# First batch of a fused attention and SwiGLU kernel: the remainder's normalization gets a chain of its own, and three late pairs move ahead of the last weight block's lead half

## The chip, the core and the metric

The kernel runs on one core of one Trainium2 chip. A core has five engines with instruction queues of their own: PE (matmuls; its weight loads are listed as PEld), DVE (vector work), ACT (activations and copies), POOL (general vector work, and here the DMAs that cast) and SP (DMAs). Each engine takes its queue in order, and they meet at semaphores. Matmuls read SBUF and write PSUM banks. The metric is the time of one execution on the device, in microseconds; lower is better.

## The reference

Linear attention without softmax, an RMS norm per head, and then a SwiGLU feed-forward layer with an RMS norm over the model width in front:

```python
kv = np.einsum('bhsd,bhse->bhde', k, v)          # 8 batches, 8 heads, 576 rows, 64 wide
out = np.einsum('bhsd,bhde->bhse', q, kv)
rms = np.sqrt(np.mean(out * out, axis=-1, keepdims=True) + 1e-06)
attn = out / rms * g_norm
x = attn.transpose(0, 2, 1, 3).reshape(B * S, H * D)      # 4608 x 512
rms = np.sqrt(np.mean(x * x, axis=-1, keepdims=True) + 1e-06)
xn = x / rms * rms_g
g = xn @ w_gate                                           # 512 x 1536
silu = g * (1.0 / (1.0 + np.exp(-g)))
return silu * (xn @ w_val) @ w_out                        # 1536 x 512
```

Inputs and output are float32; the kernel multiplies in bfloat16.

## The kernel before

The 576 rows of a batch are cut into 512 main rows (four chunks of 128, numbered 0 to 3) and a remainder of 64 rows (chunk NC = 4). The feed-forward layer runs over nine groups of 512 rows: the main rows of each of the eight batches, and one group `xr` that gathers the eight remainders. A group has twelve hidden blocks j of 128; each takes a gate product (`wg`), a silu on ACT, a val product (`wv`) and a multiply on DVE that gives `h`. Then come the products with `wo`. Both norms are merged into one factor for each row and head, `al`: a matmul with `sel` sums squares into `st`, and a chain of twelve small DVE steps (`chain`, lines 455 to 488: u, r, t, srow, z, y, then two rounds of nt, nt, al) turns the sums into the factor by an inverse square root from a bit trick (y) and two Newton rounds. `xna` is the product of attention output and factor; `xT_mm` turns it by matmuls with the identity, and `xT_out` copies it into `x` (main chunks) or `xr` (remainder).

The weights of gate and val are loaded in four blocks of three j each (`FB`), by DMAs of POOL's queue in the order wg0, wv0, wg1, wv1 up to wv3. Behind them POOL issues loads of batch 1, the four `wo` loads and loads of batch 2.

The first batch is written out by hand, in program order, with no planner. Columns of x stand for rows of the batch. Its first two chunks (256 columns, the lead half) are prepared first. Then a list `early` of 22 slots runs all of the lead half's gate and val products, and behind each slot n a function `behind(n)` (line 861) issues a piece of the work that prepares the rest of the batch, chunks 2, 3 and the remainder:

- slot 0: the gates of j 0 to 2 together; slots 1 to 3: their vals.
- slots 4 to 6 gates and 7 to 9 vals of weight block 1; 10 to 12 and 13 to 15 of block 2; 16 to 18 and 19 to 21 of block 3.
- behind 0 and 1 the transposes of q (`qT_mm`, `qT_out`; the remainder at 1); behind 2 to 4 the transposed output and its square (`oT_mm`, `sqT_`); behind 5 and 6 the sums (`stat_pairs`), all into one tile; behind 6 to 10 the twelve chain steps (`steps`) over chunks 2 to 4 at once; behind 8 to 10 the output itself (`o_pairs`); behind 12, 13 and 15 `xna`; behind 15, 16 and 18 the transposes of x and the copies on ACT.

After the list come twelve slots that each hold gate and val of one j for the late half (columns 256 to 511), and then sixteen slots of products with `wo`. The attention of batch 1 is put behind these by slot number (`place_second`, with its first argument after the planner as the slot of its k-v product); later batches and groups are placed by a planner with costs (`Placer`). Gate and val products of one slot after another rotate through three PSUM banks (`mm1`): a gate's bank is free when its silu has been taken, a val's when its h has been made.

Line 641 is the matmul of gate and val, 669 that of the first gates, 308 the transposes of q, 380 `oT_mm`, 405 the sums, 350 `o_pairs`, 520 the transposes of x, 530 and 542 the copies of x on ACT, 360 `xna`, 650 silu, 659 h, 215 the cast of the remainder of q on POOL, 466 to 484 the chain.

Of the kernel before, what the change touches and what calls it, by code (L numbers as in the profile page):

```python
# [86 lines left out]
def kernel(  # L87
# [17 lines left out]
    NC = 4  # L105
    MAIN = 128 * NC
    REM = S - MAIN
    NS = d_model // 128
    NF = d_ff // 128
    FB = (3, 3, 3, 3)  # L110
# [21 lines left out]
    o2_p = pool("o2", 2, space=bass.MemoryType.PSUM)  # L132
    att_p = pool("att", 3, space=bass.MemoryType.PSUM)
# [454 lines left out]
    def place_second(P, s):  # L588
        a = Att(1)
        V, A = nc.vector, nc.scalar  # L590
        ps = {}
        pe = lambda at, cost, n, fn: P.at("PE", cost, lambda: ps.__setitem__(n, fn()), s + at)
        dve = lambda at, cost, fn: P.at("DVE", cost, fn, s + at)
        act = lambda at, cost, fn: P.at("ACT", cost, fn, s + at)

        def turn_q():
            for n, (js, chunks) in enumerate(((P0, range(NC)), (P1, range(NC)), (ALL, (NC,)))):
                ps[n] = a.qT_heads(js, chunks)

        P.at("PE", 1.2, turn_q, s - 4)  # L600
        for j in range(2):
            dve(-3 + j, 0.42, lambda j=j: a.qT_out(ps[0][:, j : j + 1], (j,), 0, V))
            act(-3 + j, 0.58, lambda j=j: a.qT_out(ps[1][:, j : j + 1], (2 + j,), 0, A))
        act(-1, 0.58, lambda: a.qT_out(ps[2], ALL, NC, A))
        P.at("PE", 1.14, lambda: a.kv_mm(range(NS)), s)
        dve(1, 0.43, lambda: a.kv_half(0))
        dve(1, 0.43, lambda: a.kv_half(1))

        parts = [((j,), 0, NC) for j in range(NS)] + [(ALL, NC, NC + 1)]
        for n in range(NC + 1):  # L610
            pe((2, 2, 3, 4, 5)[n], 0.25, ("oT", n), lambda n=n: a.oT_mm(*parts[n]))
            act((3, 4, 4, 5, 6)[n], 0.62, lambda n=n: a.sqT_(ps["oT", n], *parts[n]))
        act(6, 1.28, lambda: A.preload_act_table(ACT.Sqrt))
        P.at("PE", 0.64, lambda: a.stat_mm(0, NC + 1), s + 6)
        for n in range(NC + 1):
            P.at("PE", 0.24, lambda n=n: a.o_mm(n, mm1_p if n == 2 else None), s + (7, 7, 8, 9, 10)[n])
        dve(7, 2.2, lambda: a.lead_chain(0, NC + 1, True))
        for c in range(NC + 1):
            dve(9 + c, 0.68, lambda c=c: a.xna_(c, V, a.o[c]))
        for at, js, cs in ((11, P0, (0, 1)), (13, P1, (0, 1)), (14, P0, (2, 3)), (15, P1, (2, 3))):  # L620
            P.at("PE", 0.24, lambda js=js, cs=cs: a.xT_mm(js, cs), s + at)
            for j in js:
                dve(at + 1, 0.3, lambda j=j, cs=cs: a.xT_out(j, cs, V))
        P.at("PE", 0.15, lambda: a.xT_mm(ALL, (NC,)), s + 16)
        dve(17, 0.62, lambda: [a.xT_out(j, (NC,), V) for j in ALL])
        P.floor = s + 18
        return s + 18
# [24 lines left out]
    def gate_of(g, j, c0=0, c1=MAIN):  # L652
        silu_of(g, j, mm1(g, wg, j, c0, c1), c0, c1)
# [7 lines left out]
    def slots_a(g, j, c0=0, c1=MAIN):  # L661
        return [Slot("gate", lambda: gate_of(g, j, c0, c1)), Slot("val", lambda: val_of(g, j, c0, c1))]

    def gates(g, js, c0, c1):
        ps = [mm1_p.tile([128, MAIN], FP32, name="mm1")[:, : c1 - c0] for _ in js]
        for s in range(NS):
            for p, j in zip(ps, js):
                n, jj = where[j]
                nc.tensor.matmul(
                    p, lhsT=wg[n][:, s, jj * 128 : (jj + 1) * 128], rhs=x_of(g, s, c0, c1), start=s == 0, stop=s == NS - 1  # L670
                )
        for p, j in zip(ps, js):
            silu_of(g, j, p, c0, c1)
# [61 lines left out]
    def slots_b_by_j(g):  # L735

        box = {}
        order = [(j, t) for j in range(NF) for t in range(4)]

        def part(n):  # L740
            if n == 0:
                for t in range(4):
                    p = o2_p if t < 2 else mm1_p
                    box[t] = p.tile([128, d_model], FP32, name="o2" if t < 2 else "mm1")
            for j, t in order[BJ * n : BJ * (n + 1)]:
                mm2(box[t], g, j, t)
            if n == 4 * PARTS - 1:
                for t in (2, 3, 0, 1):
                    store(g, t, box[t], nc.vector if t == 3 else nc.scalar)

        return [Slot("all", lambda n=n: part(n)) for n in range(4 * PARTS)]
# [12 lines left out]
    V, G, A = nc.vector, nc.gpsimd, nc.scalar  # L764
    H0, H1 = (0, 4), (4, 8)
    P0, P1 = (0, 1), (2, 3)
    ALL = range(NS)
# [32 lines left out]
    a = Att(0)  # L800
# [49 lines left out]
        f()  # L850

    half = MAIN // 2
    early = [Slot("half", lambda: gates(0, range(FB[0]), 0, half))]
    for n, w in enumerate(FB):
        js = range(FB0[n], FB0[n] + w)
        early += [slots_a(0, j, 0, half)[0] for j in js if n] + [slots_a(0, j, 0, half)[1] for j in js]
    held = {}

    steps = {6: (0, 3), 7: (3, 5), 8: (5, 8), 9: (8, 10), 10: (10, 12)}

    def behind(n):
        if n == 0:
            ps = a.qT_mm(ALL, (2, 3))
            a.qT_out(ps[:, 0:2], P0, 2, V)
            a.qT_out(ps[:, 2:4], P1, 2, V)
        elif n == 1:
            a.qT_out(a.qT_mm(ALL, (NC,)), ALL, NC, A)
        elif n in (2, 3):
            js = (P0, P1)[n - 2]
            a.sqT_(a.oT_mm(js, 2, 4, o2_p), js, 2, 4)  # L870
        elif n == 4:
            a.sqT_(a.oT_mm(ALL, NC, NC + 1, o2_p), ALL, NC, NC + 1)
        elif n == 5:
            a.st = None
            a.stat_pairs(P0, 2, 4, att_p, "att")
            a.stat_pairs(P1, 2, 4, att_p, "att")
        elif n == 6:
            a.stat_pairs(ALL, NC, NC + 1, att_p, "att")
        if n in steps:
            for f in a.chain(2, NC + 1)[slice(*steps[n])]:  # L880
                f()
        if n in (8, 9):
            held[n - 8] = a.o_pairs((P0, P1)[n - 8], 2, 4, att_p, "att")
        elif n == 10:
            held[2] = a.o_pairs(ALL, NC, NC + 1, o2_p, "o2")
        if n in (12, 13):
            i = (12, 13).index(n)
            a.xna_pairs(held[i], (P0, P1)[i], 2, 4)
        elif n == 15:
            a.xna_pairs(held[2], ALL, NC, NC + 1)  # L890
        if n in (15, 16):
            i = (15, 16).index(n)
            a.xT_mm((P0, P1)[i], (2, 3), None if i else o2_p)
            for j in (P0, P1)[i]:
                a.xT_out(j, (2, 3), A)
        elif n == 18:
            a.xT_mm(ALL, (NC,))
            for j in ALL:
                a.xT_out(j, (NC,), A)
# [11 lines left out]
    gate = load_q(2)  # L911
    tc.add_manual_dep(gate.ins, wo_loads[0].ins.name, SYNC, reason="the weights come first")

    def one(two):
        return Slot("half", lambda: [s.run() for s in two])

    slots = [one(slots_a(0, j, half, MAIN)) for j in range(NF)] + slots_b_by_j(0)
    starts = [0]
    for g in (*range(1, B - 1), B, B - 1):
        starts.append(len(slots))  # L920
        slots += [s for j in range(NF) for s in slots_a(g, j)] + slots_b(g, g == B - 1)
    P = Placer(slots, 3)
    casts = ()
    for b in range(1, B):
        if b == 1:
            end = place_second(P, 9)
        else:
            s0 = starts[b - 1]
            end = place_attention(P, b, casts, s0 - 2, s0 + 2 * NF - 4)
        if os.environ.get("PLACER"):  # L930
            print("batch", b, "to", end, "wanted at", starts[b], "casts", casts)
        else:
            assert end < starts[b] + (b == 1), (b, end, starts)
        if b == 1:
            for n, at in ((0, 6), (1, 24), (2, 30), (3, 40)):
                for j in range(NS):
                    for w, eng, cost in ((wg, "DVE", 0.09), (wv, "ACT", 0.13)):
                        f = P.put(eng, cost * FB[n], lambda w=w, n=n, j=j, e=eng: fold(w[n], j, e), at=starts[1] + at + j)
                        assert f[1] < starts[2] + (2 * FB0[n] if n == 3 else 0), f
            casts = place_casts(P, 2, starts[1] - 9)  # L940
        elif b + 1 < B:
            P.put("SP", 0.0, lambda b=b: load_q(b + 1), at=starts[b - 1] + 6 * (b == 2))
            casts = place_casts(P, b + 1, starts[b - 1] + 18)
            for n, f in enumerate(loads_kv(b + 1)):
                if b == 2:
                    P.at("POOL", 0.85, f, starts[1] + 11 + n)
                else:
                    P.put("POOL", 0.85, f, at=starts[b - 1] + 14)
# [29 lines left out]
```

## Time and profile before

| | |
|---|---|
| median of 3 runs | 325.04 us (324.96 to 325.22) |
| profiled execution | 324.99 us, span 323.2 us, granted clock 1.000 |
| busy | PE 312.9 us, DVE 178.7, ACT 143.1, POOL 89.3 |
| span of the list `early`, from its first matmul | 17.41 to 31.86 us |
| the fourth late pair's gate starts | 34.48 us |

Times of an instruction are microseconds from the start of the span. The timeline's rows read: start, time taken by the merged run of equal instructions, engine, line, operation, what is written and read, form, count, and in brackets how long the engine sat idle before and what ended that. Matmuls overlap: the time between starts is the pace, and the time taken is longer. The chain of waits follows the last instruction back to what released it; its rows read start, time, what.

### The profile page before, as it was taken

To read this page: it belongs to the slowest core of one execution; us is meant where nothing else is said; L and a number is where in the kernel's file an instruction comes from. 1 tells how busy PE (TensorE), PEld (TensorE's weight loads), DVE (VectorE), ACT (ScalarE), POOL (GpSimd) and SP (SyncE) were. 2 spreads that over 40 slices of the span, in tenths; PEclk is the share of its full clock that TensorE was granted. 3 is DMA by queue.
4 is the path that set the end of the run, shared out by engine and by line. 5 is a ranking of instruction groups with operands and counts; after the bars stand their busy time and mean duration, and the time that the engine had idled before them with its cause. 6 is when DMAs were issued, how large, how long until landed. Compare 5 with 4: busy or idle time off the path is not lost.

```text
span 323.2 us, 5403 instructions
## 1 busy us (share of the span) xinstructions
PE 312.9 (97%) x2041; PEld 162.3 (50%) x2062; DVE 178.7 (55%) x394; ACT 143.1 (44%) x266; POOL 89.3 (28%) x110
## 2 busy tenths in 40 slices
PE   5999999999999999999999999999999999999995
PEld 1678866554454445444554445444544444444443
DVE  4658438489938672857185818681778133203411
ACT  1464566485758323832283228422742233223320
POOL 8763420049016600670067005800420000000000
PEclk9999999999999999999999999999999999999999
DMA  8999999949673984499559956896000800040002
GB/s 215 220 200 198 194 223 217 220 139 147 121 199 107 139 163 140 130 124 158 144 148 108 140 150 173 90 139 162 35 1 0 172 32 0 3 108 21 0 34 97
DMA packets 78213, 40.49 MB, mean 125 GB/s; under 512 B 41960, under 2 KB 73708, under 8 KB 78188
## 3 DMA queue, kind: packets, MB, share of 16 engines
q0 software_dynamic: 30672, 14.16, 34.2%
q1 hardware_dynamic: 46032, 25.01, 31.8%
q10 hardware_dynamic: 1484, 0.99, 1.0%
q8 instruction: 16, 0.26, 0.3%
q14 instruction: 9, 0.07, 0.1%
HBM read 37.78 MB, written 9.44 MB: 146 GB/s over the span
## 4 chain that ended last, share of the span: by engine, by line
PE 89%; DMA 5%; ACT 2%; issue 1%; DVE 1%; POOL 0%; SPq 0%; ACTq 0%; POOLq 0%
PE mm L641 55%; PE o L676 26%; DMA rstg<-in_q_dram 3%; DMA remv<-in_v_dram 2%; PE att L341 2%; PE att L273 2%; PE mm L676 1%; PE o L706 1%; ACT sq L367 0%; PE att L520 0%; ACT silu L650 0%; DVE h L659 0%; PE att L319 0%; ACT outa L371 0%; ACT wv L795 0%
## 5 line engine op out<-in xcount | busy, mean ns | idle before, releaser
L659 DVE TENSOR_TENSOR h<-silu,mm 128x512 bf16<-128x512 bf16 (+1 forms) x120 | 75.7, 631 | 82.4 <-PE mm L641 75.9
L650 ACT ACTIVATE silu<-mm 128x512 bf16<-128x512 f32 (+1 forms) x120 | 66.3, 556 | 82.5 <-PE mm L641 73.3
L641 PE MATMUL mm<-x,wv 128*128 128x512 bf16 (+1 forms) x431 | 99.8, 355 | 0.1
L641 PE MATMUL mm<-x,wg 128*128 128x512 bf16 (+1 forms) x419 | 98.5, 358 | 0.2 <-DVE h L659 0.2
L676 PE MATMUL o<-wo,h 128*128 128x512 bf16 x383 | 87.6, 379 | 1.3 <-issue 0.8
L422 POOL TENSOR_TENSOR sq<-sq,g 128x512 bf16<-128x512 bf16 x30 | 34.6, 1155 | 130.8 <-ACT sq L367 130.7
L641 PEld LDWEIGHTS <-wv 128*128 128x128 bf16 x480 | 46.2, 98 | 44.0
L641 PEld LDWEIGHTS <-wg 128*128 128x128 bf16 x468 | 44.7, 98 | 42.9 <-issue 0.6
L676 PEld LDWEIGHTS <-h 128*128 128x128 bf16 x420 | 40.2, 98 | 46.0 <-DVE h L659 0.2
L692 ACT COPY osb<-o 128x512 f32<-128x512 f32 x33 | 19.3, 587 | 69.4 <-PE o L676 69.4
L427 DVE TENSOR_REDUCE st<-sq 128x8 f32<-128x512 bf16 x60 | 38.8, 678 | 1.1 <-ACT sq L367 0.8
L302 DVE CAST kvs<-att 64x256 bf16<-64x256 f32 x14 | 5.9, 422 | 30.3 <-PE att L273 30.2
L367 ACT ACTIVATE sq<-att 128x512 bf16<-128x512 f32 x30 | 17.9, 598 | 2.2 <-PE att L341 2.2
L494 DVE TENSOR_TENSOR xna<-outa,al 128x512 bf16<-128x512 bf16 x30 | 18.7, 682 | 0.0
L371 ACT CAST outa<-att 128x512 bf16<-128x512 f32 x30 | 17.7, 590 | 0.0
L341 PEld LDWEIGHTS <-qTs 128*128 128x128 bf16 x140 | 10.2, 98 | 6.9
L641 PE MATMUL mm<-xr,wg 128*128 128x512 bf16 x47 | 12.3, 379 | 0.1
L641 PE MATMUL mm<-xr,wv 128*128 128x512 bf16 x47 | 12.3, 379 | 0.1
L341 PE MATMUL att<-kvs,qTs 128*128 128x128 bf16 x136 | 12.2, 219 | 0.0
L208 POOL CAST main_q<-stg 128x1024 bf16<-128x1024 f32 (+1 forms) x12 | 11.3, 976 | 0.7 <-DMA stg<-in_q_dram 0.7
L237 PE MATMUL mm<-idle 128*128 128x512 bf16 x26 | 7.5, 452 | 4.0 <-DVE idle L163 4.0
L795 ACT ACTIVATE wv<-wv,gain 128x384 bf16<-128x384 bf16 x16 | 9.2, 611 | 0.5 <-PE mm L641 0.5
(132 smaller groups left out, 174.5 us busy)
## 6 DMA issues: line engine op xcount, KB each, us to landing
out_dram<-osb SPq DMA_DIRECT2D x31, 256.0 KB, 2.6
stg<-in_q_dram SPq DMA_DIRECT2D x6, 1024.0 KB, 7.0
vc<-in_v_dram POOLq DMA_DIRECT2D x7, 512.0 KB, 8.3
kc<-in_k_dram POOLq DMA_DIRECT2D x7, 512.0 KB, 6.1
wg<-in_moe_w_gate_dram POOLq DMA_DIRECT2D x4, 384.0 KB, 15.6
wv<-in_moe_w_val_dram POOLq DMA_DIRECT2D x4, 384.0 KB, 16.8
wo<-in_moe_w_out_dram POOLq DMA_DIRECT2D x4, 384.0 KB, 13.2
out_dram<-osb SPq DMA_DIRECT2D x8, 128.0 KB, 2.3
```

What stands on the lines that cost most here:

```text
L208: return copy(out=mains[b, t][:, cs[0] : cs[1], h0:h1, :], in_=staged[b, t].rearrange("p h (c d) -> p c h d", c=NC)[:, cs[0] : cs[1], h0:h ...
L341: nc.tensor.matmul(o[:, 2 * j : 2 * j + 2, :], lhsT=self.qTj[:, j, c, :], rhs=self.kv[:, j, :, :], start=j == 0, stop=j == NS - 1, skip_gr ...
L367: nc.scalar.activation(out=self.sq[c][:, 0], in_=self.o[c], func=ACT.Square)
L371: (eng.tensor_copy if eng else nc.scalar.copy)(out=self.outa[c], in_=self.o[c])
L422: eng.tensor_tensor(out=self.sq[c][:, 1], in0=self.sq[c][:, 0], in1=g2, op=OP.mult)
L427: nc.vector.reduce_sum(out=self.st[:, which, c, :], in_=self.sq[c][:, which], axis=AX.X)
L494: return eng.tensor_tensor(out=self.xna[:, c], in0=src, in1=self.al[:, c, :].to_broadcast([128, H, D]), op=OP.mult)
L641: nc.tensor.matmul(ps[:, : c1 - c0], lhsT=w[n][:, s, jj * 128 : (jj + 1) * 128], rhs=x_of(g, s, c0, c1), start=s == 0, stop=s == NS - 1)
L650: nc.scalar.activation(out=sis[g, j][:, c0:c1], in_=ps, func=ACT.Silu)
L659: nc.vector.tensor_tensor(out=hs[g, j][:, c0:c1], in0=sis[g, j][:, c0:c1], in1=v_ps, op=OP.mult)
L676: nc.tensor.matmul(ps, lhsT=hs[g, j][:, t * 128 : (t + 1) * 128], rhs=wo[j // OB][:, j % OB, :], start=j == 0, stop=j == NF - 1)
L692: (eng.copy if eng is nc.scalar else eng.tensor_copy)(out=o, in_=ps)
```

## The change

The remainder of the first batch leaves the chain of chunks 2 and 3. The main chain now covers chunks 2 and 3, and its steps stand behind slots 5 to 9. The remainder's transposes of q move from behind slot 1 to behind slot 9, its transposed output and square from 4 to 15, its sums from 6 to 16 into a tile of their own, its output from 10 to 17; it gets the twelve chain steps a second time, for one chunk, behind slots 17 to 20, its `xna` moves from 15 to 21 and its transposes of x from 18 to 23. The main `xna` and transposes of x come one slot sooner (11, 12 and 14, 15), the main sums are split over slots 4 and 5.

The late half's slots are made ahead of the list, and the first three of them (j 0 to 2, weight block 0) are put into `early` ahead of weight block 3: they are now slots 16 to 18, block 3's gates 19 to 21 and its vals 22 to 24. The list after it holds nine late slots, and batch 1's placement starts at slot 6 where it started at 9.

```diff
     half = MAIN // 2
+
+    def one(two):
+        return Slot("half", lambda: [s.run() for s in two])
+
+    late = [one(slots_a(0, j, half, MAIN)) for j in range(NF)]
     early = [Slot("half", lambda: gates(0, range(FB[0]), 0, half))]
     for n, w in enumerate(FB):
         js = range(FB0[n], FB0[n] + w)
+        if n == len(FB) - 1:
+            early += late[: FB[0]]
         early += [slots_a(0, j, 0, half)[0] for j in js if n] + [slots_a(0, j, 0, half)[1] for j in js]
     held = {}
 
-    steps = {6: (0, 3), 7: (3, 5), 8: (5, 8), 9: (8, 10), 10: (10, 12)}
+    steps = {5: (0, 3), 6: (3, 6), 7: (6, 8), 8: (8, 10), 9: (10, 12)}
+    rsteps = {17: (0, 3), 18: (3, 6), 19: (6, 9), 20: (9, 12)}
 
     def behind(n):
         if n == 0:
             ps = a.qT_mm(ALL, (2, 3))
             a.qT_out(ps[:, 0:2], P0, 2, V)
             a.qT_out(ps[:, 2:4], P1, 2, V)
-        elif n == 1:
-            a.qT_out(a.qT_mm(ALL, (NC,)), ALL, NC, A)
         elif n in (2, 3):
             js = (P0, P1)[n - 2]
             a.sqT_(a.oT_mm(js, 2, 4, o2_p), js, 2, 4)
-        elif n == 4:
-            a.sqT_(a.oT_mm(ALL, NC, NC + 1, o2_p), ALL, NC, NC + 1)
-        elif n == 5:
-            a.st = None
-            a.stat_pairs(P0, 2, 4, att_p, "att")
-            a.stat_pairs(P1, 2, 4, att_p, "att")
-        elif n == 6:
-            a.stat_pairs(ALL, NC, NC + 1, att_p, "att")
+        elif n in (4, 5):
+            if n == 4:
+                a.st = None
+            a.stat_pairs((P0, P1)[n - 4], 2, 4, att_p, "att")
         if n in steps:
-            for f in a.chain(2, NC + 1)[slice(*steps[n])]:
+            for f in a.chain(2, 4)[slice(*steps[n])]:
                 f()
-        if n in (8, 9):
-            held[n - 8] = a.o_pairs((P0, P1)[n - 8], 2, 4, att_p, "att")
-        elif n == 10:
-            held[2] = a.o_pairs(ALL, NC, NC + 1, o2_p, "o2")
-        if n in (12, 13):
-            i = (12, 13).index(n)
-            a.xna_pairs(held[i], (P0, P1)[i], 2, 4)
-        elif n == 15:
-            a.xna_pairs(held[2], ALL, NC, NC + 1)
-        if n in (15, 16):
-            i = (15, 16).index(n)
+        if n in (7, 8):
+            held[n - 7] = a.o_pairs((P0, P1)[n - 7], 2, 4, att_p, "att")
+        elif n == 9:
+            a.qT_out(a.qT_mm(ALL, (NC,), o2_p), ALL, NC, A)
+        elif n in (11, 12):
+            a.xna_pairs(held[n - 11], (P0, P1)[n - 11], 2, 4)
+        elif n in (14, 15):
+            if n == 15:
+                ps = a.oT_mm(ALL, NC, NC + 1, o2_p)
+            i = n - 14
             a.xT_mm((P0, P1)[i], (2, 3), None if i else o2_p)
             for j in (P0, P1)[i]:
                 a.xT_out(j, (2, 3), A)
-        elif n == 18:
+            if n == 15:
+                a.sqT_(ps, ALL, NC, NC + 1)
+        elif n == 16:
+            a.st = None
+            a.stat_pairs(ALL, NC, NC + 1, att_p, "att")
+        if n in rsteps:
+            for f in a.chain(NC, NC + 1)[slice(*rsteps[n])]:
+                f()
+        if n == 17:
+            held[2] = a.o_pairs(ALL, NC, NC + 1, o2_p, "o2")
+        elif n == 21:
+            a.xna_pairs(held[2], ALL, NC, NC + 1)
+        elif n == 23:
             a.xT_mm(ALL, (NC,))
             for j in ALL:
                 a.xT_out(j, (NC,), A)
...
-    def one(two):
-        return Slot("half", lambda: [s.run() for s in two])
-
-    slots = [one(slots_a(0, j, half, MAIN)) for j in range(NF)] + slots_b_by_j(0)
+    slots = late[FB[0] :] + slots_b_by_j(0)
...
         if b == 1:
-            end = place_second(P, 9)
+            end = place_second(P, 6)
```

## The prediction

> **What bounds the kernel now.** I first read the busy table of the profile page, then the chain of waits between 17 and 32 us, and then the timeline of PE, DVE and POOL in the same stretch. The lines, in that order:
>
> ```profile
> PE 312.9 (97%) x2041; PEld 162.3 (50%) x2062; DVE 178.7 (55%) x394; ACT 143.1 (44%) x266; POOL 89.3 (28%) x110
> ...
> 19.40 0.62 POOL remq L215
> 20.02 0.04 issue
> 20.07 0.40 PE att L308 x4
> ...
> 26.19 0.41 DVE L659 TENSOR_TENSOR h<-silu,mm 128x256 bf16<-128x256 bf16 x1
> 26.66 0.60 PE L641 MATMUL mm<-x,wg 128*128 128x256 bf16 x4 [0.19 <-DVE h L659]
> 28.40 0.39 PE L520 MATMUL o<-ident,xna 128*128 128x128 bf16 x4
> 28.62 0.60 PE L641 MATMUL mm<-x,wg 128*128 128x256 bf16 x4
> 28.82 0.84 ACT L530 ACTIVATE x<-o,gain 128x256 bf16<-128x256 bf16 x2 [1.15 <-PE o L520]
> 29.58 0.68 DVE L360 TENSOR_TENSOR xna<-o,al 128x512 bf16<-128x512 f32 x1
> 30.48 1.55 PE L641 MATMUL mm<-x,wv 128*128 128x256 bf16 x12
> 34.48 0.60 PE L641 MATMUL mm<-x,wg 128*128 128x256 bf16 x4
> ...
> 24.98 0.88 POOL L194 DMA_DIRECT2D kc<-in_k_dram  x1 [1.30 <-DMA wg<-in_moe_w_gate_dram]
> 26.88 0.69 POOL L190 DMA_DIRECT2D kc<-in_k_dram  x1 [1.02 <-DMA wv<-in_moe_w_val_dram]
> 28.78 0.75 POOL L232 DMA_DIRECT2D wo<-in_moe_w_out_dram  x1 [1.21 <-DMA wg<-in_moe_w_gate_dram]
> 30.71 0.76 POOL L232 DMA_DIRECT2D wo<-in_moe_w_out_dram  x1 [1.19 <-DMA wv<-in_moe_w_val_dram]
> 33.63 0.76 POOL L232 DMA_DIRECT2D wo<-in_moe_w_out_dram  x1 [2.16 <-DMA qc<-in_q_dram]
> 25.24 0.60 DVE L475 TENSOR_SCALAR y<-z 128x24 int32<-128x24 int32 x1
> ```
>
> PE is 97% busy, so only its gaps can be won or added. From the starts of successive matmuls (four of 256 columns take 0.44 us, four of 128 take 0.22, four statistics 0.11) I read the time PE lost between the first gates (17.41) and the fourth late pair (the gate at 34.48): 0.46 before 20.07 (the remainder of q, cast on POOL), 0.36 before 26.66 (a PSUM bank held by h, whose multiply sits in the chain's queue on DVE), 0.10 before 29.38, 0.06 before 30.32, 0.03 before 30.48 and 0.07 inside those val matmuls. Together 1.08 us. After 34.48 I find no wait on an engine or a transfer: what is left are steps of about 0.1 us at changes of matmul shape, and 0.22 us holes that come back in each batch and are as long as one 512-column matmul (0.216); the table shows 21 fewer matmuls than weight loads, so I take these for missing records. So a shift of the matmul at 34.48 reaches the end whole.
>
> The POOL lines show a second limit. Each such issue reuses the semaphore of an earlier load, and starts 0.28 to 0.29 us after that load's last semaphore update in the trace. The updates of wv of block 1, wg and wv of block 2, wg and wv of block 3 are at 22.70, 24.69, 26.60, 28.50 and 30.43. PE's gates of block 3 start at 28.62 and its vals at 30.48: PE now follows the weights, so an earlier PE would have met them.
>
> **The change, part by part.** (n is a slot of the early list; after it come the steps "behind" it.)
>
> *The remainder's transposes leave n=1.* The 0.46 us wait goes. Late next are weights. I lay PE's new order out with the durations above. Gates 17.41, transposes 18.72, then val 0, val 1, oT, val 2, oT, gate 3, four statistics, gate 4, four statistics, gate 5 end at 22.46; q's copies (DVE, done at 20.13), the squares and h do not hold this. Val 3 needs wv of block 1: landing 22.70 plus 0.05 (30.43 to 30.48) is 22.75, a wait of 0.29. Val 3 to 5, two o-groups and the remainder's transposes, now at n=9, take PE to 24.72. Gate 6 waits 0.02 for wg of block 2 and gates 6 to 8 end at 26.05. Val 6 needs wv of block 2, 26.65: a wait of 0.60.
>
> *The main chain covers 16 numbers in a row of the tile, not 24, and starts one slot sooner, at n=5.* It starts at about 22.13 on DVE. Steps follow each other by 0.20 to 0.22 us (0.29 to 0.34 after the reciprocal; an independent h only 0.10 after the step before it). Its last h, of val 5, ends near 25.15, or 25.5 if y takes 0.60 as now; gate 8 needs it by 25.62 and val 6 waits for weights till 26.65 anyhow. Cost nothing; the cover is val 6's wait. Without it, each tenth would show.
>
> *The three late pairs move ahead of block 3's lead half.* They need the x of chunks 2 and 3, which ACT writes behind n=14 and n=15. Let Z be the end of val 7, 26.65+0.88=27.53. Then xT of pairs 0,1 (0.22), val 8 (0.44), the remainder's oT (0.22), xT of pairs 2,3 (0.22): PE is at the first late gate at Z+1.10. ACT starts 0.42 after such a transpose starts (28.40 to 28.82); the second group starts at Z+0.88, so its two copies start at Z+1.30 and Z+1.67 (pitch 0.37) and the last ends at Z+2.15 (0.48). The matmul that reads it starts at Z+2.21, the gate ends at Z+2.32 where it would have ended at Z+1.54. Cost 0.78, in the open. Before, 2.5 us of other matmuls lay between. That a matmul waits for its own slice of x only is shown at 17.41, where gates start before the last x copy ends (17.97). The square of the remainder's oT, queued on ACT behind those copies, ends at about Z+2.61, and the first late silu behind it; the statistics stand at Z+2.76, so both fit. The gain of this part is that wg and wv of block 3, needed at about Z+5 now, landed long before.
>
> *The remainder gets a chain of its own (12 more DVE steps), late.* PE from the statistics: 0.11, late pair 1 (0.875), the remainder's o (0.22), and late pair 2 starts its val at L = Z+4.40. DVE takes its queue in order: h of pair 1, steps 1 to 3, then h of pair 2, which starts 0.71 us after its first matmul (33.17 to 33.88 in the late rows), L+0.71. Then steps 4 to 12: the first 0.33 later, eight more by 0.20, then xna: it starts at L+0.71+0.33+1.80=L+2.84 and ends after 0.68; PE may start the remainder's xT at L+3.58. PE has only val, gates 9 to 11, vals 9 and 10 in between: 6 times 0.4375, so it stands there from L+2.62. Cost 0.96 in the open. Behind the waiting xT stand val 11 and everything after; behind xna on DVE stand h of vals 9 and 10, which end 0.2 us before their banks are wanted.
>
> The width of this chain, 8 numbers, has no row; the lead chain's 16 (14.59, 14.80, 15.00: 0.20 apart) and the 24 here bound a step between about 0.17 and 0.22. I take 0.20, the nearest row; nine steps then give plus or minus 0.25 us, within which the cost lies between 0.7 and 1.15.
>
> *Queues and placement.* SP's broadcast of g keeps its place at n=12 and waits for block 3's gates as before. The load of batch 2's q waits for the first output weights, at 41.97, and POOL's two squares of g came at 41.78 behind its own loads; neither is set by the early list's length. Batch 1's work is placed from slot 6 instead of 9 in a list that is three shorter: the same matmuls. Cost nothing.
>
> **Sum.** Waits after: 0.29+0.02+0.60+0.78+0.96=2.65; before 1.08. The difference, +1.57 us, moves the gate now at 34.48 to about 36.05 and the end with it. The profiled execution took 324.99 us (its span of 323.2 and 1.8 around it), 0.05 below the median, 325.04; so 326.6 by either.
>
> **Rivals.** *A step of the remainder's chain is held by POOL.* In the trace y (SBUF to SBUF, a tensor-scalar) takes 0.60 at 25.24 and ends at 25.84, with POOL's issue of 24.98 to 25.86; the six y without POOL work beside them take 0.18. The u at 79.09, also SBUF to SBUF, takes 0.77 beside a POOL cast that ends at 79.81. The new y would start at L+1.44=33.37 and end at 33.55; POOL's issue starts at 33.63 and lasts to 34.39. If PE is 0.26 us later than I reckon, y ends at 34.39, 0.85 later: +2.4, 327.45. The nearness speaks for it, the order of my sum against it. [...]
>
> *One of the two new waits is covered.* If matmuls run ahead of the x copies less tightly, or DVE passes steps faster, one of 0.78 and 0.96 goes: +0.79 or +0.61, 325.65 to 325.8. Against it: both follow from in-order queues with durations in the rows.
>
> *Given back later, not slower.* If the 0.22 holes at 44.81, 50.09, 56.83, 64.33 and 71.93 are waits for transfers or other timed work rather than missing records, a later PE finds them over: they sum to 1.1, which leaves about +0.45, 325.5, no measurable difference; it decides from 0.92 given back on. Against it: no releaser is named, and the count of records explains them.
>
> *The move pays.* Both waits covered leaves only the weights' 0.91 against 1.08: -0.17, 324.9. A measurable gain would need the weights early as well, at most -1.08, 324.0. The landings do not depend on PE, so I give this little.
>
> **How the numbers follow.** The plain sum 0.55 (its own range 326.2 to 327.0: the chain's steps, 0.25, and landings of some 0.15), POOL's hold 0.17, one wait covered 0.15, given back 0.06, the move pays without a measurable gain 0.04, with one 0.03. A measurement tells about 0.2%, 0.65 us, from no change. Slower by more holds the first two and about two thirds of the third: 0.82; same 0.15; faster 0.03. The range 325.6 to 327.5 takes in the first three, 0.87.
>
> **What would show it.** In the changed profile: no wait for the cast of the remainder of q near 20; val 3 and val 6 starting just after the POOL issues' loads landed, near 22.75 and 26.65; a PE gap of some 0.8 in the first late gate near 29, ended by ACT's x of L530; one of some 1.0 before the remainder's xT near 34.6, ended by DVE's xna; no wait for block 3's weights; the same matmul pace afterwards. The prediction is wrong if either gap is missing, if y is held, or if the matmuls after 36 catch up.

## The result and the profile after

The changed kernel takes 326.96 us (median; 326.68 to 327.31) where the kernel before, run beside it, takes 325.00. The ratio is 1.0051, 95% interval 1.0037 to 1.0065: slower by 0.5%. The profiled execution took 327.05 us with a span of 325.3, 2.1 longer than the span before. One execution of 1175.05 us (in all_covered) and one of 1886.52 us (of the kernel before, beside it) lie far off all others and are in no ratio below.

The timeline of PE in the changed kernel (start, time taken, what, and in brackets idle time and what ended it) has both new gaps:

```profile
18.36 1.47 PE L669 MATMUL mm<-x,wg 128*128 128x256 bf16 x12
...
25.35 1.69 PE L641 MATMUL mm<-x,wg 128*128 128x256 bf16 x12
27.14 1.05 PE L641 MATMUL mm<-x,wv 128*128 128x256 bf16 x8
...
29.13 0.48 PE L641 MATMUL mm<-x,wg 128*128 128x256 bf16 x2
29.85 0.63 PE L641 MATMUL mm<-x,wg 128*128 128x256 bf16 x2 [0.25 <-ACT x L530]
30.32 0.60 PE L641 MATMUL mm<-x,wv 128*128 128x256 bf16 x4
...
34.14 1.04 PE L641 MATMUL mm<-x,wv 128*128 128x256 bf16 x8
35.99 0.29 PE L520 MATMUL att<-ident,xna 128*128 128x64 bf16 x4 [0.81 <-DVE xna L360]
36.12 0.60 PE L641 MATMUL mm<-x,wv 128*128 128x256 bf16 x4
36.55 0.60 PE L641 MATMUL mm<-x,wg 128*128 128x256 bf16 x4
```

The bracket counts idle time after the modelled end of a matmul. What PE lost is read from the starts: the first late gate begins at 29.13 and its val at 30.32, 1.19 for a piece of work that takes 0.44 elsewhere. That is a loss of 0.75; added up from the single steps between its matmuls (0.10, 0.41, 0.26) it is 0.77, the figure used below. Vals 9 and 10 begin at 34.14 and take 0.87, and the remainder's transposes begin at 35.99: 0.98 lost. The fourth late pair's gate is the row at 36.55; it was at 34.48.

The same stretch of DVE and POOL says who was late:

```profile
32.01 0.42 DVE L659 TENSOR_TENSOR h<-silu,mm 128x256 bf16<-128x256 bf16 x1 [0.56 <-PE mm L641]
...
33.10 0.42 DVE L659 TENSOR_TENSOR h<-silu,mm 128x256 bf16<-128x256 bf16 x1 [0.16 <-PE mm L641]
33.44 0.15 DVE L471 TENSOR_REDUCE srow<-t 128x1 f32<-128x8 f32 x1
33.63 0.17 DVE L472 SCALAR_TENSOR_TENSOR z<-srow,u 128x8 f32<-128x8 f32 x1
33.83 0.17 DVE L475 TENSOR_SCALAR y<-z 128x8 int32<-128x8 int32 x1
34.03 0.17 DVE L482 TENSOR_TENSOR nt<-y 128x8 f32<-128x8 f32 x1
...
35.04 0.17 DVE L484 SCALAR_TENSOR_TENSOR al<-nt,al 128x8 f32<-128x8 f32 x1
35.24 0.69 DVE L360 TENSOR_TENSOR xna<-o,al 128x512 bf16<-128x512 f32 x1
...
27.37 0.69 POOL L190 DMA_DIRECT2D kc<-in_k_dram  x1 [1.03 <-DMA wv<-in_moe_w_val_dram]
34.12 1.51 POOL L232 DMA_DIRECT2D wo<-in_moe_w_out_dram  x2 [2.15 <-DMA qc<-in_q_dram]
```

Steps 4 to 12 of the remainder's chain follow each other by about 0.20 us from 33.44 to 35.04 (four of the rows are left out), xna starts 1.80 after the first of them and ends at 35.93, and PE starts 0.06 later. The POOL row at 27.37 again stands 0.28 us after the landing of a load: wv of block 2 landed at 27.09 and its first matmul is the one at 27.14.

The ledger of what PE lost in this profile, from the first gates to the fourth late pair, is 0.22 for a bank before gate 8, 0.26 for wv of block 2, 0.77 for x and 0.98 for the remainder, together 2.23 us; before it was 1.08. That is +1.15. The other 0.95 of the 2.1 is that the first gates start at 18.36 and not at 17.41, though nothing ahead of them is changed. The first question for the runs was therefore whether that late start belongs to the change.

### The profile page after: what moved, and what is told of

Same layout as the page of the kernel before. It is cut to its first block, busy times and chain, and to the rows that moved or that the text cites. A ratio compares the mean times of both kernels' runs of the same rounds, so it can differ in the third digit from the quotient of the medians.

```text
span 325.3 us, 5436 instructions
## 1 busy us (share of the span) xinstructions
PE 315.8 (97%) x2062; PEld 162.4 (50%) x2062; DVE 179.8 (55%) x406; ACT 143.4 (44%) x266; POOL 89.2 (27%) x110
## 4 chain that ended last, share of the span: by engine, by line
PE 89%; DMA 8%; DVE 1%; issue 1%; ACT 0%; DVEq 0%; POOLq 0%
PE mm L641 55%; PE o L676 26%; DMA wv<-in_moe_w_val_dram 6%; PE att L341 2%; DMA remv<-in_v_dram 2%; PE att L273 2%; PE mm L676 2%; PE o L706 1%; PE att L520 0%; PE att L319 0%; PE att L380 0%; DVE xna L360 0%; PE mm L706 0%; ACT x L530 0%; PE att L415 0%
## 5 line engine op out<-in xcount | busy, mean ns | idle before, releaser
L676 PE MATMUL o<-wo,h 128*128 128x512 bf16 x396 | 90.1, 379 | 0.0
L237 PE MATMUL mm<-idle 128*128 128x512 bf16 x27 | 8.7, 490 | 4.0 <-DVE idle L163 4.0
```

Source lines behind the costliest of these rows:

```text
L676: nc.tensor.matmul(ps, lhsT=hs[g, j][:, t * 128 : (t + 1) * 128], rhs=wo[j // OB][:, j % OB, :], start=j == 0, stop=j == NF - 1)
```

## The experiments

Theory: the landing of block 2's val weights sets a floor for PE, and behind it stand two waits, for x at the first late gate and for the remainder's chain on DVE. All ratios are to the kernel before, run beside on the same chip.

**The changed kernel again (after_again).** No edit.

> The changed kernel once more, unchanged. Theory (the block 2 val weights set a floor, and two new PE waits come behind it): about 326.9, 1.9 above the kernel before; a PE gap of 0.75 to 0.8 in the first late gate and of 0.95 to 1.0 before the remainder's transposes of x; from the first val of weight block 2 to the fourth late pair's gate 9.4 us again, whenever the first gates start. Rival (the late start of the first gates, 18.36 instead of 17.41, belongs to the change and is half of the loss): the first gates start near 18.4 again and the two gaps alone do not give the difference.

Measured: 326.68 us, ratio 1.0052 (1.0040 to 1.0064). Its PE timeline:

```profile
17.47 1.47 PE L669 MATMUL mm<-x,wg 128*128 128x256 bf16 x12
...
23.11 0.61 PE L641 MATMUL mm<-x,wv 128*128 128x256 bf16 x4 [0.47 <-ACT silu L650]
...
27.03 1.05 PE L641 MATMUL mm<-x,wv 128*128 128x256 bf16 x8 [0.40 <-DMA wv<-in_moe_w_val_dram]
```

Here the first gates start at 17.47, 0.89 sooner, and the profiled execution still takes 326.92 us: PE stands 0.63 before the first val of block 1 and 0.57 before that of block 2. The weights of these vals landed at 23.07 and 26.99. The bracket at 23.11 names a silu that ended at 23.06, but in the first profile the same val began 0.20 before that silu started, so it does not need it. From the first val of block 2 to the fourth late pair's gate the two profiles take 9.41 and 9.42 us. The rival falls: an early start is spent on waiting for weights.

**x sooner (x_sooner).** The transposes of pairs 2 and 3 join those of 0 and 1 behind slot 14, and DVE copies them beside ACT:

```diff
...
-            i = n - 14
-            a.xT_mm((P0, P1)[i], (2, 3), None if i else o2_p)
-            for j in (P0, P1)[i]:
-                a.xT_out(j, (2, 3), A)
...
+            for i in range(2):
+                a.xT_mm((P0, P1)[i], (2, 3), None if i else o2_p)
+                for j in (P0, P1)[i]:
+                    a.xT_out(j, (2, 3), (A, V)[i])
...
```

> Only the x of pairs 2 and 3 comes sooner: turned behind slot 14 together with pairs 0 and 1, and copied by DVE beside ACT. Theory: the 0.77 us gap in the first late gate goes to under 0.1, the gap before the remainder's transposes stays at 0.9 to 1.0 because its chain moves along with the late pairs, and the time falls by 0.6 to 0.8 from the changed kernel, to about 326.2. Rival (the remainder's chain is anchored to something that does not move with PE, so one gap swallows the other): the second gap grows to about 1.7 and the time stays at 326.9.

Measured: 326.15 us, ratio 1.0036 (1.0024 to 1.0048). No gap is left in the first late gate, and the one before the remainder's transposes is 0.98, unchanged. By the two medians of the changed kernel, 326.96 and 326.68, the wait for x was worth 0.5 to 0.8 us, about what it showed, and the chain moves with the pairs.

**The remainder's transposes later (rem_later).** Two more late pairs go into the list, and the transposes stand behind slot 26:

```diff
+    early += late[FB[0] : FB[0] + 2]
...
-        elif n == 23:
+        elif n == 26:
             a.xT_mm(ALL, (NC,))
...
```

> Only the remainder's transposes of x move: from behind slot 23 to behind slot 26, two late pairs being put in between. Theory: PE has 2.2 us more of its own work before them, so the 0.98 us gap goes; the first gap stays at 0.77; about 325.9 to 326.0. Rival (DVE is behind, and the gap only turns into waits for PSUM banks that h of vals 9 and 10 holds): gaps of together about 1 us at the fourth and fifth late pair, and 326.9.

Measured: 326.81 us, ratio 1.0051 (1.0038 to 1.0063). The theory was wrong here, and its rival right. DVE, then PE, of this run:

```profile
35.71 0.69 DVE L360 TENSOR_TENSOR xna<-o,al 128x512 bf16<-128x512 f32 x1
36.32 1.07 DVE L659 TENSOR_TENSOR h<-silu,mm 128x256 bf16<-128x256 bf16 x3
35.27 0.82 PE L641 MATMUL mm<-x,wv 128*128 128x256 bf16 x6
36.78 0.60 PE L641 MATMUL mm<-x,wg 128*128 128x256 bf16 x4 [0.70 <-DVE h L659]
```

Three h stand behind xna on DVE, and the next gate needs the bank that the first of them frees: 0.86 lost at 36.78 instead of 0.98 before the transposes. This points to how much DVE work stands together as what made the wait, and not to who asks for the result; rem_spread below tests it.

**Both edits (both_covered).**

> Both edits together. Theory: neither gap, about 325.2, within 0.2% of the kernel before: what the change wins by dropping the wait for the remainder's cast it pays back at the weights of block 2. Rival (the two waits are not the whole price, for instance the first gates start later because of the change): 325.9 or more.

Measured: 325.80 us, ratio 1.0035 (1.0020 to 1.0049). The x gap is down to one step of 0.10, the 0.87 us bank wait stays. So x_sooner's gain and rem_later's lack of one add up, but this expectation, made before rem_later was seen, was missed by 0.6.

**Each part alone (pairs_only, rem_only).** The first moves the three late pairs and leaves the remainder in the main chain:

```diff
+        if n == len(FB) - 1:
+            early += late[: FB[0]]
...
-        elif n == 15:
+        elif n == 17:
             a.xna_pairs(held[2], ALL, NC, NC + 1)
-        if n in (15, 16):
-            i = (15, 16).index(n)
+        if n in (14, 15):
+            i = (14, 15).index(n)
...
-        elif n == 18:
+        elif n == 20:
             a.xT_mm(ALL, (NC,))
...
```

> One part of the change alone: the three late pairs ahead of block 3's lead half, the remainder left in the main chain of 24 numbers (its xna and transposes two slots later, the main transposes one slot sooner). Theory: the waits for the cast of the remainder of q (0.4) and for the bank before gate 8 (0.3) are there as in the kernel before, block 3's weights are no longer waited for, and the first late gate waits 0.8 to 1.2 us for x; no wait of 0.98 before the remainder's transposes. About 325.7 to 326.2. Rival (the pairs' move is what costs, not the second chain): 326.7 or more.

Measured: 326.00 us, ratio 1.0018 (1.0010 to 1.0027). Its PE timeline has 0.63 before the remainder's transposes of q, 0.36 before gate 8, 0.43 for xna before the two transposes of x, and 0.77 in the first late gate:

```profile
20.23 0.40 PE L308 MATMUL att<-ident,remq 128*128 128x128 bf16 x4 [0.46 <-POOL remq L215]
26.81 0.60 PE L641 MATMUL mm<-x,wg 128*128 128x256 bf16 x4 [0.19 <-DVE h L659]
30.17 0.63 PE L641 MATMUL mm<-x,wg 128*128 128x256 bf16 x2 [0.29 <-ACT x L530]
```

The second keeps the remainder's own chain at its slots and puts the three late pairs behind block 3's lead half:

```diff
-        if n == len(FB) - 1:
-            early += late[: FB[0]]
         early += [slots_a(0, j, 0, half)[0] for j in js if n] + [slots_a(0, j, 0, half)[1] for j in js]
+    early += late[: FB[0]]
```

> The other part alone: the remainder has its own chain at the same slots as in the changed kernel, but block 3's lead half stands ahead of the three late pairs. Theory: no wait for x in the first late gate; block 3's vals meet their weights (0.2 to 0.4), and the remainder's chain, now among the h of vals 9 to 11, holds banks or the transposes for 0.5 to 1.1 us in all; about 325.8 to 326.4. Rival (the second chain costs nothing once the pairs are away): 325.3 or less.

Measured: 326.38 us, ratio 1.0033 (1.0021 to 1.0045). The time is as expected, the waits only in part. The first late gate no longer waits for x, but the remainder's statistics, behind slot 16, come 0.4 us sooner in PE's queue, and their square stands on ACT behind the copies of x; ACT's two rows and the PE row:

```profile
28.91 0.84 ACT L530 ACTIVATE x<-att,gain 128x256 bf16<-128x256 bf16 x2
29.64 0.60 ACT L391 ACTIVATE sqT<-o 128x512 bf16<-128x512 f32 x1
30.29 0.25 PE L405 MATMUL att<-sel,sqT 128*128 128x4 bf16 x4 [0.98 <-ACT sqT L391]
```

PE loses 1.15 there, 0.25 more before the val at 33.49 and 0.11 before the remainder's transposes. Block 3's weights, expected to be waited for, have landed by then. Each part alone is slower than the kernel before.

**The chain spread thin (rem_spread).** With x_sooner's edit, two chain steps behind each of slots 17 to 21, the rest among the late pairs after the list:

```diff
-    rsteps = {17: (0, 3), 18: (3, 6), 19: (6, 9), 20: (9, 12)}
+    rsteps = {17: (0, 2), 18: (2, 4), 19: (4, 6), 20: (6, 8), 21: (8, 10)}
...
+    P.at("DVE", 0.4, lambda: [f() for f in a.chain(NC, NC + 1)[10:12]], 0)
+    P.at("DVE", 0.68, lambda: a.xna_pairs(held[2], ALL, NC, NC + 1), 1)
+    P.at("PE", 0.12, lambda: a.xT_mm(ALL, (NC,), o2_p), 3)
+    P.at("ACT", 0.56, lambda: [a.xT_out(j, (NC,), A) for j in ALL], 7)
...
```

> The changed kernel with the sooner x of the run x_sooner, and the remainder's chain spread thin: two steps behind each of slots 17 to 21, the last two in the first slot after the list, xna in the second, the transposes after the fourth late pair of that list. Theory: the 0.87 us bank wait that the run with both edits kept came from DVE being given chain, xna and h at once; spread, neither gap is left, and the time is 324.7 to 325.2. Rival (DVE has too much work in this stretch wherever it stands): a bank wait of 0.4 or more again, and 325.4 or more.

Measured: 325.02 us, ratio 0.9995 (0.9987 to 1.0004). Both gaps are gone; from the first late gate at 29.10 to the fourth pair's at 34.66 PE never stops:

```profile
29.10 0.60 PE L641 MATMUL mm<-x,wg 128*128 128x256 bf16 x4
...
32.05 1.47 PE L641 MATMUL mm<-x,wg 128*128 128x256 bf16 x12
33.35 1.47 PE L641 MATMUL mm<-x,wv 128*128 128x256 bf16 x12
34.66 0.60 PE L641 MATMUL mm<-x,wg 128*128 128x256 bf16 x4
```

So the two waits are the loss of the change: without them it is level with the kernel before, within an interval of about 0.3 us to either side.

**The floor (no_block2_wait, rem_spread_fill).** One test takes one wait for weights away from the changed kernel: the lead half's vals of block 2 read the val weights of block 1, which landed 3.8 and 3.9 us sooner in the two profiles of the changed kernel. All loads stay, but the values of that half are no longer the reference's.

```diff
-        v_ps = mm1(g, wv, j, c0, c1)
+        v_ps = mm1(g, wv, j - 3 if g == 0 and c0 == 0 and c1 < MAIN and 6 <= j < 9 else j, c0, c1)
```

> The changed kernel, but the lead half's vals of block 2 (j 6 to 8 of the first batch) read block 1's val weights, which landed 3.6 us sooner; all loads stay. So the values of the first batch's lead half are not the reference's, and the time is that of a kernel without this one wait for weights. Theory (the landing of block 2's val weights is the floor under the changed kernel when the first gates start early): the first val of block 2 starts right after gate 8, the two later gaps stay at 0.77 and 0.98, and the time falls by 0.25 to 0.6, to 326.1 to 326.5. Rival (the floor is the later work on DVE and ACT, which those vals do not release): no change, 326.7 to 326.9.

Measured: 326.07 us, ratio 1.0033 (1.0022 to 1.0044), 0.6 to 0.9 below the changed kernel's two medians, a little more than the expected end. The first val of block 2 starts at 26.19, before its own weights' landing at 26.53, with no wait, and the two gaps behind it are 0.77 and 0.98 as ever. The landing is the floor under the changed kernel. Not all of the fall is the edit's: by this profile's own landing the val could have started near 26.58, so 0.39 is won there, and the rest of the distance to 27.03 and 27.14 is that the weights came sooner in this execution.

The other moves the remainder's oT, o and statistics ahead of that val in rem_spread, to use the wait:

```diff
         elif n in (11, 12):
+            if n == 11:
+                a.sqT_(a.oT_mm(ALL, NC, NC + 1, o2_p), ALL, NC, NC + 1)
             a.xna_pairs(held[n - 11], (P0, P1)[n - 11], 2, 4)
+            if n == 12:
+                held[2] = a.o_pairs(ALL, NC, NC + 1, o2_p, "o2")
+                a.st = None
+                a.stat_pairs(ALL, NC, NC + 1, att_p, "att")
...
```

> As rem_spread, and the remainder's oT, statistics and o products, 0.55 us of PE, moved from behind slots 15 to 17 to behind 11 and 12, ahead of the first val of block 2 that waits for its weights. Theory (the weights' landing sets the floor there): the work fills that wait, and the time falls by 0.3 to 0.5 more, to 324.3 to 324.8, below the kernel before. Rival (PE is not held by the weights there): the same time as rem_spread.

Measured: 324.94 us, ratio 0.9994 (0.9985 to 1.0003), short of the expectation. The profile has no wait for block 2's val weights any more, but 0.25 for the square before the statistics and 0.33 for x in the first late gate, which now has 0.22 less work of PE in front of it. It also waits 0.42 for block 1's val weights.

**A version that beats both (all_covered, fewer_spins, before_fewer_spins).** all_covered takes rem_spread_fill, puts the statistics behind slot 13 and the transposes of x behind 13 and 14, with each pair's copies shared by ACT and DVE.

> As rem_spread_fill, with the statistics behind slot 13 and the transposes of x behind slots 13 and 14, each pair's two copies shared by ACT and DVE. Theory (PE's work before the block 2 vals fills the wait for their weights, and x and the remainder are ready when asked): the 0.25 us wait for the square and the 0.33 us for x that rem_spread_fill had are gone, and the time is 324.3 to 324.7, faster than the kernel before by 0.1 to 0.25%. Rival (the time is set by when the first gates start, which moves by chance between 17.3 and 19.1): the same median as rem_spread_fill, 324.9 to 325.1.

Measured: 325.17 us, ratio 1.0002 (0.9991 to 1.0013): close to the rival's outcome. Five of its executions took 324.65 to 324.80 us and six 325.08 to 325.94. In the profiled one, of 324.75, the first gates start at 17.87, the square is not waited for and x still costs 0.35. My reading is that the six had a late start, which no wait behind it takes up any more; none of them was profiled, so no trace shows it. The idle matmuls that open the kernel took 7.42 us in the first profile of the changed kernel where they took 6.49 in the one of before, and its first gates came 0.95 later, so the next run has four fewer of them:

```diff
-    spin(mm1_p.tile([128, MAIN], FP32, name="mm1"), 18)
+    spin(mm1_p.tile([128, MAIN], FP32, name="mm1"), 14)
```

> As all_covered, with 14 instead of 18 idle matmuls at the very start (line 799). In the traces so far these follow each other by 0.43 us for the first 3.0 to 5.3 us and by 0.22 after, and the first gates start between 17.3 and 19.1 with that. Theory (in an execution where the fast pace comes late, the idle matmuls themselves hold back the first real ones, and with no wait for weights left this reaches the end): four fewer end 0.9 us sooner at worst, the first gates start at 17.3 to 17.9, the times no longer spread over 1.2 us, and the median is 324.5 to 324.9, faster than the kernel before by 0.1 to 0.2%. Rival (the real matmuls at the slow pace cost as much as the idle ones did, or the fast pace comes later still without them): the same spread, and 325.0 or more.

Measured: 324.85 us, 324.61 to 324.98 in eleven executions, ratio 0.9984 (0.9975 to 0.9993). The first gates start at 17.46 in its profile, and PE then waits 0.59 before the first val of block 1, whose weights landed at 23.02: an earlier start than this would gain nothing there. The run is faster than the kernel before by 0.16%, and than the changed kernel by 0.6 to 0.7%. The same edit alone on the kernel before:

> The kernel before with 14 instead of 18 idle matmuls at the start, and nothing else. Theory (the kernel before stands behind the cast of the remainder of q near 20 us and behind block 3's weights near 30.5, so most of a late start is taken up there): the median stays within 0.1% of the kernel before, at 324.9 to 325.2, and what fewer_spins won is not won by this edit alone. Rival (the four idle matmuls cost the kernel before as much): 324.7 or less.

Measured: 325.02 us, ratio 0.9994 (0.9985 to 1.0003). So the edit alone makes no difference that is clear of noise. But the two intervals overlap, so how the 0.16% divides between this edit and the order of the work is not shown. Nor do the waits of the kernel before (the cast of the remainder, block 3's weights) seem to take up a late start whole: its fifteen executions beside this run spread over 0.98 us, up to 325.77, and the eleven with four fewer idle matmuls over 0.44, up to 325.27.

## Why the prediction was right, and where it was off

The direction was right, and so was the mechanism: both new waits are there, with the size that was worked out. For x 0.78 was predicted and 0.77 measured in both profiles of the changed kernel; for the remainder 0.96 was predicted, 0.98 and 0.97 measured. The stretch from the first val of block 2 to the fourth late pair's gate was to be 9.42 us (26.65 to about 36.07, by adding up its steps) and is 9.41 and 9.42. The step width of 0.20 us for the chain of 8 numbers, taken between 0.17 and 0.22, is what DVE's rows show. The wait for the cast of q's remainder is gone, block 3's weights are not waited for, and the main chain costs nothing, all as stated.

The term that was mis-sized is the landing of block 2's val weights. I took 26.60 from the one profile of before, with some 0.15 about it; in the two profiles of the changed kernel it landed at 27.09 and 26.99. That is the 0.4 to 0.5 us by which the gate at 36.55 (36.45 in the repeat) misses the predicted 36.05, and about the 0.36 by which the median, 326.96, lies over 326.6. The repeat's median, 326.68, is only 0.08 over, so the profiled executions may have had a later landing than most. In the profiles of the ten edited kernels from x_sooner to fewer_spins it landed at 26.41 to 26.77. Of these, rem_later, rem_only and x_sooner run the same program as the changed kernel up to this landing, and there it came at 26.41, 26.67 and 26.69. So I take the two late ones for chance; what sets the landing no run shows.

The order of the waits for weights was right only for an early start. The repeat has 0.63 and 0.57 at the vals of blocks 1 and 2 against 0.29 and 0.60; the first profile starts 0.95 later and has 0 and 0.26. The 0.22 for a bank before gate 8 there is covered, as was said of the main chain: without it PE would have waited 0.48 for the weights. The sum does not depend on any of this, since the landing sets where PE goes on.

Of the rivals, POOL's hold of y did not come about. In the first profile y ran from 33.83 to 34.00 and POOL's issue began at 34.12, which is near the 0.08 that was reckoned; in the repeat the issue began at 34.66, so the distance is not fixed, and that it was enough was in part luck. But a nearer issue need not have cost anything. In rem_later y starts inside an issue and is not held:

```profile
34.30 0.17 DVE L475 TENSOR_SCALAR y<-z 128x8 int32<-128x8 int32 x1
33.67 1.51 POOL L232 DMA_DIRECT2D wo<-in_moe_w_out_dram  x2 [2.37 <-DMA qc<-in_q_dram]
```

Over all profiles of this document thirteen y of the first batch ran beside an issue of POOL. Two took 0.59 to 0.60 (before and pairs_only), one 0.27 (no_block2_wait) and ten 0.17 to 0.18, one of them in before_fewer_spins, at 25.20 beside an issue of 24.96 to 25.85. So a y that starts inside an issue need not pay the rival's price, and that it then ends with the issue was my reading of one y of before (25.84 beside 25.86) and one u beside a cast (79.86 beside 79.81); what decides is not shown.

"Given back later" is ruled out: the after page lists 2062 matmuls to 2062 weight loads, and the 0.22 us holes are not in its trace; they were missing records. The repeat, with 2041 records, has them again, all later by the same shift: the hole of before at 44.81 is at 46.78, and that at 309.44 is at 311.40.

```profile
PE 315.8 (97%) x2062; PEld 162.4 (50%) x2062; DVE 179.8 (55%) x406; ACT 143.4 (44%) x266; POOL 89.2 (27%) x110
```

"One wait covered" and "the move pays" were made true by hand in the experiments. With x ready the ratio falls from 1.0052 to 1.0036; with both covered and DVE spread it is 0.9995, and the -0.17 reckoned for that case lies inside its interval. What I had wrong about this came after the prediction: that the remainder's wait would go if only its transposes came later.

## What to carry to other kernels

When work is taken out of one engine's wait and put later, lay out the queue of every engine that it passes through, and count from the instruction that releases it to the first one that reads it. Here nine steps of 0.20 us and one of 0.68 stood against 2.2 us of matmuls. A consumer moved later does not help if the producer's queue also frees the banks (rem_later lost 0.86 us where 0.98 had been lost); the small dependent steps have to be spread into the idle time between the big ones (rem_spread lost nothing there).

## What the runs showed of the hardware

The late start of the first gates comes from the pace of the idle matmuls at the very start, 512 columns each: the first product behind them starts at 10.31 in the profile before and at 11.25 in that of the changed kernel, 0.94 later, and the first gates at 17.41 and 18.36, 0.95 later. The matmul rows, before first and the changed kernel second:

```profile
3.99 6.49 PE L237 MATMUL mm<-idle 128*128 128x512 bf16 x22 [3.99 <-DVE idle L163]
...
17.41 1.47 PE L669 MATMUL mm<-x,wg 128*128 128x256 bf16 x12
```

```profile
3.99 7.42 PE L237 MATMUL mm<-idle 128*128 128x512 bf16 x22 [3.99 <-DVE idle L163]
```

They follow each other by 0.43 us at first and by 0.22 later. The change of pace comes 3.0 us after the first one in the profile before and 5.1 in that of the changed kernel; over all profiles it comes between 2.5 (rem_spread_fill) and 5.5 us (rem_later, whose first gates start at 19.10). The granted clock is listed as 1.00 at both paces (4 to 7 and 7 to 10 us of the profile before, 4 to 9 and 9 to 11 of the changed kernel's). From one execution to the next the change moves by 3 us; what sets its moment no run here shows. With four idle matmuls fewer the times of fewer_spins spread over 0.37 us; those of all_covered, with all of them, over 1.3.

The landing of block 2's val weights moves by 0.7 us between the profiled executions (26.41 to 27.09 for the same load behind the same loads), more than the whole effect of some edits here; one profile is a thin basis for a floor.
